# Attention ahead of two expert stages: full-row third score product, a shorter prologue, spread loads and splits

## The chip, the cores and the metric

The kernel runs on one core of a Trainium2 chip. The metric is the device time of one execution in microseconds (us), the median of several runs. Five engines work beside each other, each through its own list of instructions in order: TensorE (PE; weight loads are shown as PEld), VectorE (DVE), ScalarE (ACT), GpSimd (POOL) and SyncE (SP), which here issues the DMAs. Semaphores are the only order between engines.

## The reference

Three stages run in a row; only the first is touched by the change. It is attention with a position bias, over 2 batches, 8 heads, 576 positions and 64 columns per head:

```python
scores = scale * np.matmul(q, k.transpose(0, 1, 3, 2))
x = (psi_rel / psi_i)[..., None]            # from |i-j| and i
bias = np.maximum(x @ w1 + b1, 0.0) @ w2    # 32 hidden, one value per head
scores = scores + bias.transpose(2, 0, 1)[None]
attn = softmax(scores);  out = attn @ v
```

Then follow an MoE stage (1152 rows, 8 experts, 512 to 1024 to 512 columns) and an FFN (512 to 2048 to 512). Everything is float32.

## The kernel before, in words

A float32 product on TensorE is built from products of split operands: each operand is rounded to a short form ("h") and the rest is kept ("l"), and three of the products of parts are summed. For the scores the first two are one: a 128-row operand qs holds for each head h the rounded q in its 64 rows and q's rest in the other 64 rows, and meets kh, k's rounded copy in both halves. So one product over 128 rows yields two of the three. The third, q rounded with k's rest, is a product over 64 rows with kl.

Attention runs until about 214 us. A **block** is a pair of heads and a batch (8 blocks), a **step** is one block with one tile t of query rows (128 rows, or 64 for t = 4): 40 steps. The first four blocks go together, tile 4 first (steps 0 to 3), then tiles 0 to 3 of all four (steps 4 to 19); then come two groups of two blocks (steps 20 to 39).

Each step is written out by hand, one letter of an order string for each piece: R and S reduce the scores of the two heads with the bias (VectorE, L1213), E and F take the exponential (ScalarE, L1228), N norms (VectorE, and a spread of the reciprocals on POOL, L1239), T, U and V transpose the previous step's result, a is one of the five pieces of the value product (av, L1282, L1285, L1295), X writes the result back, Q is the next step's score product (sc, L1198 with kh, L1203 with kl). M, O and H are the bias: 36 **groups** of 16 rows, for each of which H computes four hidden rows ht (VectorE L1390 or ScalarE L1388), M multiplies them (TensorE, L1406), O scales them out and stores them to scr in HBM (L1441); L loads bias tiles bt of a step pair back from there (L1181). The string is ORD_A while bias groups are left, ORD_B after. A p takes one piece of a block's preparation (prep: two casts on VectorE, L1159, then subtractions on POOL, L1164 for qs and L1165 for kl) and two items of a background list.

The background list holds the splits of the first MoE weights (w_split, queued at steps 27 and 28; sums on POOL L302, copies on ScalarE L315, subtractions on VectorE L316) and of the first MoE operand (ops_first, queued at steps 35 and 37; POOL L332, ScalarE L352, VectorE L353).

Ahead of the steps stands a prologue of 12 groups, in which blocks 0, 1 and 2 are prepared (queued at groups 0, 2 and 6). The raw q and k of a block come by four DMAs into a ring of three places (load_qk). All DMAs are in SP's queue, in order. The MoE and FFN stages are ordered by a planner, from costs, after the attention; its inputs are the same before and after.

Of the kernel before, what the change touches and what calls it, by code (L numbers as in the profile page):

```python
# [7 lines left out]
F32 = mybir.dt.float32  # L8
# [14 lines left out]
HALF = S // 2  # L23
# [6 lines left out]
NB = 2  # L30
LAG = 1
TO = [4, 0, 1, 2, 3]
QB = 5
AB = 2
BD = 1
PRE = 12
PH = [0, 2, 6]
LQ = [4, 11, 105, 114, 116, 121]
LV = [1, 2, 3, 4, 20, 19, 32, 28]
ACC = [2.6, 3.1]  # L40
WARM = 8
PS = [[3, 0], [4, 12], [5, 16], [6, 19], [7, 25]]
ORD_A = "RXTSMOHUapaEaaNpFaLMOVQH"
ORD_B = "RTSNUXaafLEafappFVQa"
TOFF = [0, 128, 256, 384, 512]
TROW = [128, 128, 128, 128, 64]
NN = [256, 320]
# [172 lines left out]
def attention_moe_elu_ffn_kernel(  # L220
# [83 lines left out]
    def w_split():  # L304
        (kind, he, j), t = raw_q.pop(0)
        hi, lo = wt0[he, j] = w1_new()
        st = stp.tile([128, 4, 2, 128], F32, tag="st", name="st")

        def sums():
            for i in range(4):  # L310
                w1_sum(t, st, i, pool)

        def part(i):
            dst, src = w1_src(t, st)[i]
            act.activation(out=hi[:, dst], in_=src, func=ACTF.Copy)  # L315
            dve.tensor_tensor(out=lo[:, dst], in0=src, in1=hi.bitcast(F32)[:, dst], op=ALU.subtract)  # L316

        bg.extend([sums] + [lambda i=i: part(i) for i in range(4)] + [raw_load])

    def ops_new(n):  # L320
        p = xp if n == 0 else pools["ops1"]
# [19 lines left out]
    def ops_first(t):  # L341
        if not ops0:
            ops0.extend(ops_new(0))
        oh, ol = ops0
        i0, i1 = XPAIR[t]
        xa, xb = ops_view(0, t, xt[i0], xt[i1])
        c = slice(128 * t, 128 * t + 128)
        st = stp.tile([128, 4, 2, 128], F32, tag="st", name="st")

        def part(i):  # L350
            o, src = ops_src(xa, xb, st)[i]
            act.activation(out=oh[:, o, :, c], in_=src, func=ACTF.Copy)  # L352
            dve.tensor_tensor(out=ol[:, o, :, c], in0=src, in1=oh.bitcast(F32)[:, o, :, c], op=ALU.subtract)  # L353

        def sums(i):
            ops_sum(xa, xb, st, i, pool)
            ops_sum(xa, xb, st, i + 1, pool)

        bg.extend([lambda: sums(0), lambda: sums(2)] + [lambda i=i: part(i) for i in range(4)])

    plan = Plan(0.1)
    eng = {"A": act, "D": dve, "P": pool, "S": sp}
# [745 lines left out]
    left = ctx.enter_context(ExitStack())  # L1108

    def attention(fill):  # L1110
        qkp = sb("qk", QB, left)
        vpool = sb("v", 4, right, "right")
        ep = sb("e", LAG + 2, right, "right")
        atp = sb("attnT", AB, right, "right")
# [1 line left out]
        xfp = sb("xf", LAG + 1, right, "right")  # L1116
        bp = sb("bias", NB, left)
        up = sb("u", 1, left)
        op = sb("o", 4, left)
        ring = [xp.tile([128, 3, 2, S], F32, tag=t, name="ring") for t in ("oh0", "ol0")]  # L1120

        loaded = {}
# [10 lines left out]
        def load_qk(i):  # L1133
            hp, b = blocks[i]
            loaded[i] = []
            for src, rt in ((qt, ring[0]), (kt, ring[1])):
                r = rt[:, i % 3]
                for o in (0, 64):
                    sp.dma_start(out=r[o:o + 64], in_=src[b, hp])
                loaded[i].append(r)  # L1140

        def load_v(i):
            hp, b = blocks[i]
# [8 lines left out]
        def prep(i):  # L1152
            qs = qkp.tile([128, 2, S], F32R, tag="qs", name="qs")
            kh = qkp.tile([128, 2, S], F32R, tag="kh", name="kh")
            kl = qkp.tile([128, S], F32R, tag="kl", name="kl")
            prepped[blocks[i]] = qs, kh, kl
            qr, kr = loaded.pop(i)
            for dst, src in ((qs, qr), (kh, kr)):
                dve.tensor_copy(dst, src)  # L1159
                load["d"] += 0.73  # L1160
                yield
            for h in range(2):
                o, u = slice(64 - 64 * h, 128 - 64 * h), slice(64 * h, 64 * h + 64)
                pool.tensor_tensor(out=qs[o, h], in0=qr[o, h], in1=qs.bitcast(F32)[o, h], op=ALU.subtract)  # L1164
                pool.tensor_tensor(out=kl[u], in0=kr[u, h], in1=kh.bitcast(F32)[u, h], op=ALU.subtract)  # L1165
                yield

        def prep_next():
# [15 lines left out]
        def emit_qk(s):  # L1184
            hp, b, t = steps[s]
            qs, kh, kl = prepped[hp, b]
            r = TROW[t]
            etile[s] = (
                ep.tile([128, 2 * S], F32, tag="e", name="et"),
                tp.tile([128, 2], F32, tag="nmx", name="nmx"),  # L1190
                tp.tile([128, 2], F32, tag="sm", name="sm"),
            )
            sc = [psA("sc") for _ in range(2)]
            qc = slice(TOFF[t], TOFF[t] + r)
            for h in range(2):
                for x in range(2):
                    kc = slice(HALF * x, HALF * x + HALF)
                    pe.matmul(sc[h][0:r, x, 0:HALF], qs[:, h, qc], kh[:, h, kc], start=True, stop=False)  # L1198
            for x in range(2):
                for h in range(2):  # L1200
                    kc = slice(HALF * x, HALF * x + HALF)
                    hs = slice(64 * h, 64 * h + 64)
                    pe.matmul(sc[h][0:r, x, 0:HALF], qs[hs, h, qc], kl[hs, kc], start=False, stop=True)  # L1203
            for h in range(2):
                scs[s, h] = sc[h]

# [112 lines left out]
        def run_step(s):  # L1319
            d = s - LAG  # L1320
            cur, tr = s < NS, 0 <= d < NS
            for x in ORD_A if no[0] < GRP else ORD_B:
                if x == "T" and tr:
                    emit_tr(d, 0)
                elif x == "U" and tr:
                    emit_tr(d, 1)
                elif x == "V" and tr:
                    emit_trl(d)
                elif x == "Q" and s + 1 < NS:
                    emit_qk(s + 1)  # L1330
                elif x in "RS" and cur:
                    emit_ttr(s, "RS".index(x))
                elif x in "EF" and cur:
                    emit_exp(s, "EF".index(x))
                elif x == "N" and 1 <= s <= NS:
                    emit_norm(s - 1)
                elif x == "X":
                    x_evac()
                elif x == "a":
                    av(1)  # L1340
                elif x == "M":
                    bias_p()
                elif x == "O":
                    bias_o()
                elif x == "H":
                    bias_hh()
                elif x == "p":
                    prep_next()
                    do_bg(2)
                elif x == "L":  # L1350
                    bias_loads(s)
                elif x == "f":
                    fill_pe(s)
            if tr:
                av_q.extend(av_pieces(d))
# [6 lines left out]
            pe.matmul(wp[:, 0:128], ones, ones, start=True, stop=True)  # L1362
        sp.dma_start(out=csb, in_=cst)
        sp.dma_start(out=U, in_=lext)
        load_qk(0)
        load_qk(1)
        dve.tensor_scalar(bpsi, bpsi, csb[:, C_B1:C_B1 + 1], None, ALU.mult)
        dve.tensor_scalar(U, U, csb[:, C_W1:C_W1 + 1], None, ALU.mult)

# [46 lines left out]
        def bias_out():  # L1416
            g, ps = mq.pop(0)
            r0 = 16 * g
            mid = r0 + 15
            o = op.tile([128, S + 15], F32, tag="o", name="o")  # L1420
# [47 lines left out]
        for i in range(PRE):  # L1468
# [3 lines left out]
                bias_p(True)  # L1472
            bias_loads(0)
            if i in LQ:
                load_qk(2 + LQ.index(i))
# [5 lines left out]
        bias_o()  # L1481
        emit_qk(0)
        for s in range(NS + LAG):
            if 100 + s in LQ:
                load_qk(2 + LQ.index(100 + s))
            if s in LV:
                load_v(LV.index(s))
            for i, s0 in PS:
# [104 lines left out]
```

## Time and profile before

| what | us |
|---|---|
| median of 3 runs | 1208.25 (1206.49 to 1209.31) |
| the profiled execution | 1207.91 |
| its span | 1206.1 |
| PE busy | 1170.9 (97%) |
| DVE busy | 916.1 (76%) |
| ACT busy | 626.4 (52%) |
| POOL busy | 92.9 (8%) |

Rows of the trace carry the engine, the line of the kernel, the operation, out<-in and the shape, and a time in us unless a column says ns. In a timeline, the first column is the start and the second the stretch to the end of the last instruction of the row; rows of pipelined work overlap a little, so the distance from one start to the next is what a piece takes.

### The profile page before, as it was taken

What the parts mean: (1) busy time and instruction counts of PE and PEld (TensorE: products, weight loads), DVE (VectorE), ACT (ScalarE), POOL (GpSimd) and SP (SyncE); (2) the same over time, 40 slices, a digit from 0 to 9 for tenths busy, and PEclk for the clock granted to TensorE, in tenths of its full rate; (3) what the DMA queues carried; (4) which work ended last, traced back from release to release, by engine and by line L of the source; (5) the groups of instructions that cost most, each with busy time, mean ns of one, the idle gap of its engine ahead of it and who ended that gap; (6) DMA issues with size and microseconds to landing.
All of it is one profiled execution on the core that took longest, in us unless ns stands there. A gap on an engine that the chain in (4) does not pass through costs nothing.

```text
span 1206.1 us, 19661 instructions
## 1 busy us (share of the span) xinstructions
PE 1170.9 (97%) x7432; PEld 986.9 (82%) x7432; DVE 916.1 (76%) x1932; ACT 626.4 (52%) x1413; POOL 92.9 (8%) x107
## 2 busy tenths in 40 slices
PE   7899999999999999999999999999999988999998
PEld 3467777788888888888888888888888876788887
DVE  8987787664587778778788787787776468788875
ACT  6797667554333444443434444444434346777763
POOL 4402453000000000000000000000000001000000
PEclk9999999899999999999999999999999999999999
DMA  8767741111112233242232323232411101111102
GB/s 227 221 213 200 208 122 35 33 56 53 36 36 79 80 88 102 67 129 76 92 106 88 105 87 104 90 100 68 130 45 53 53 1 36 53 53 36 36 1 79
DMA packets 36285, 104.78 MB, mean 87 GB/s; under 512 B 4064, under 2 KB 4192, under 8 KB 36192
## 3 DMA queue, kind: packets, MB, share of 16 engines
q1 hardware_dynamic: 36192, 103.54, 28.5%
q8 instruction: 58, 0.95, 0.3%
q14 instruction: 35, 0.29, 0.1%
HBM read 81.88 MB, written 21.64 MB: 86 GB/s over the span
## 4 chain that ended last, share of the span: by engine, by line
PE 91%; DVE 3%; ACT 1%; POOL 1%; issue 0%; DMA 0%; ACTq 0%; DVEq 0%
PE y L717 41%; PE m L530 38%; PE av L1285 3%; PE tr L1254 2%; PE bps L1406 2%; PE sc L1198 1%; PE sc L1203 1%; PE av L1295 1%; PE trl L1266 1%; PE av L1282 1%; PE lg L873 0%; DVE ol L353 0%; DVE et L1213 0%; DVE w1l L316 0%; DVE ol L430 0%
## 5 line engine op out<-in xcount | busy, mean ns | idle before, releaser
L530 PE MATMUL m<-oh,w1h 128*128 128x256 f32 (+1 forms) x1120 | 335.8, 300 | 3.8 <-DVE c L562 1.4
L530 PE MATMUL m<-oh,w1l 128*128 128x256 f32 (+1 forms) x1120 | 330.6, 295 | 3.8 <-ACT u L543 1.6
L530 PE MATMUL m<-ol,w1h 128*128 128x256 f32 (+1 forms) x1120 | 330.3, 295 | 2.6 <-DVE c L562 1.3
L717 PE MATMUL y<-w2h,hh 128*128 128x512 f32 x720 | 284.6, 395 | 2.9 <-ACT hh L637 1.5
L717 PE MATMUL y<-w2h,hl 128*128 128x512 f32 x720 | 283.4, 394 | 0.0
L717 PE MATMUL y<-w2l,hh 128*128 128x512 f32 x720 | 282.5, 392 | 0.8 <-DVE w2l L430 0.8
L530 PEld LDWEIGHTS m<-oh,w1h 128*128 128x128 f32 x1120 | 211.0, 188 | 45.8 <-ACT u L543 13.3
L530 PEld LDWEIGHTS m<-ol,w1h 128*128 128x128 f32 x1120 | 211.4, 189 | 22.4 <-DVE c L562 1.9
L530 PEld LDWEIGHTS m<-oh,w1l 128*128 128x128 f32 x1120 | 211.3, 189 | 5.6 <-ACT u L543 2.3
L717 PEld LDWEIGHTS y<-w2h,hh 128*128 128x128 f32 x720 | 135.1, 188 | 18.8 <-ACT hh L637 2.3
L717 PEld LDWEIGHTS y<-w2h,hl 128*128 128x128 f32 x720 | 135.1, 188 | 17.8
L543 ACT ACTIVATE p<-m 128x256 f32<-128x256 f32 (+1 forms) x160 | 65.8, 411 | 161.3 <-PE m L530 157.3
L717 PEld LDWEIGHTS y<-w2l,hh 128*128 128x128 f32 x720 | 135.2, 188 | 16.2 <-DVE w2l L430 1.4
L543 ACT ACTIVATE u<-m 128x256 f32<-128x256 f32 (+1 forms) x160 | 65.9, 412 | 132.0 <-PE m L530 128.7
L593 ACT ACTIVATE hh<-c 128x512 fp32r<-128x512 f32 (+3 forms) x128 | 72.1, 563 | 109.7 <-DVE c L562 109.6
L748 DVE SCALAR_TENSOR_TENSOR acc<-y,P,acc 128x512 f32<-128x512 f32 x126 | 94.5, 750 | 37.3 <-PE y L717 35.4
L596 DVE SCALAR_TENSOR_TENSOR hl<-c,hh 128x512 fp32r<-128x512 f32 (+3 forms) x128 | 77.5, 605 | 20.4 <-ACT hh L593 18.6
L562 DVE TENSOR_TENSOR c<-m,u 128x256 f32<-128x256 f32 (+1 forms) x80 | 36.6, 458 | 73.7 <-PE m L530 72.0
L1213 DVE CUSTOM_DVE_ANT_0 et<-sc,bt 128x576 f32<-128x576 f32 (+1 forms) x80 | 57.9, 751 | 22.0 <-PE sc L1203 17.3
L332 POOL TENSOR_TENSOR st<-xt,st 128x256 f32<-128x256 f32 (+1 forms) x8 | 6.7, 835 | 755.2 <-DVE st L332 755.0
L1228 ACT ACTIVATE et<-et,nmx 128x576 f32<-128x576 f32 (+1 forms) x80 | 61.3, 771 | 3.2 <-DVE nmx L1213 3.1
L423 ACT ACTIVATE w2h<-raw 128x512 fp32r<-128x512 f32 x80 | 48.6, 625 | 21.7 <-PE y L717 12.4
(136 smaller groups left out, 1600.1 us busy)
## 6 DMA issues: line engine op xcount, KB each, us to landing
raw<-w1p SPq DMA_DIRECT2D x32, 512.0 KB, 3.6
raw<-w2p SPq DMA_DIRECT2D x32, 512.0 KB, 3.6
scr<-o SPq DMA_DIRECT2D x36, 295.5 KB, 3.5
bt<-scr SPq DMA_DIRECT2D x16, 576.0 KB, 4.9
cw<-w1d SPq DMA_DIRECT2D x16, 512.0 KB, 4.4
wsc<-ca SPq DMA_DIRECT2D x32, 256.0 KB, 4.4
cw<-w2d SPq DMA_DIRECT2D x16, 512.0 KB, 4.4
raw<-wsc SPq DMA_DIRECT2D x16, 512.0 KB, 3.6
```

The lines of the kernel that those rows point to most:

```text
L423: act.activation(out=dst(bh.get()), in_=src(), func=ACTF.Copy)
L530: lambda e, w=w, o=o, j=j, k=k: pe.matmul(x["ap"](bank), w.get()[:, ai, j, :], o.get()[:, bi, j, :], start=(k == 0 and i in (1, 2, 5)), st ...
L543: lambda e: act.activation(out=b.get()[:, 0:N], in_=x["ap"](bank), func=ACTF.Copy),
L562: lambda e: eng[e].tensor_tensor(out=blk(b.get()[:, half * N:half * N + N], rev), in0=ap(p), in1=ap(q), op=ALU.add),
L593: op([("A", cA(w))], lambda e: act.activation(out=hh(), in_=ap(), func=ACTF.Relu), r=sk, w=wh, after=gate_)
L596: lambda e: dve.scalar_tensor_tensor(out=bl.get()[:, d], in0=ap(), scalar=0.0, in1=hhf(), op0=ALU.max, op1=ALU.subtract),
L717: lambda e, a=a, w=w, f=f, i=i, y=y, c=c: pe.matmul(y.get(), a.get()[:, c], w.get(), start=(f == 0 and i == 0), stop=(f == 3 and i == 2)),
L748: lambda e: dve.scalar_tensor_tensor(out=a.get(), in0=y.get(), scalar=P[0][:, n, e_:e_ + 1], in1=a.get(), op0=ALU.mult, op1=ALU.add),
L1213: dve.tensor_tensor_reduce(out=e.rearrange("p (x j) -> p x j", x=2), in0=sc[0:r, :, 0:HALF], in1=biast[hp, t][0:r, h].rearrange("p (x j) - ...
L1228: act.activation(out=e, in_=e, func=ACTF.Exp, scale=-1.0, bias=nmx[0:r, h:h + 1], accum_out=sm[0:r, h:h + 1])
L1254: pe.transpose(p[:, 128 * j:128 * j + r], et[0:r, c0:c0 + 128], ident[0:r, 0:r])
L1285: pe.matmul(p[64 * h:64 * h + 64, 0:r], vt[:, j - 1, 64 * h:64 * h + 64], a[:, 4 * h + j - 1, 0:r], start=False, stop=(j == 4), skip_group ...
```

## The change

The third score product runs over all 128 rows: kl holds both heads' halves in the same layout as kh, its two POOL subtractions cover 128 partitions each, and the preparation has six pieces. The prologue has 8 groups and prepares blocks 0 and 1; steps 0 to 2 have an order of their own with three groups each, and blocks 2 and 3 are prepared wholly within steps 1 and 2, three pieces at each p. Blocks 4 to 7 are loaded by one DMA per step. In ORD_B the last value piece stands ahead of V and Q. A p takes one background item, and each item does the subtraction of the part before beside the copy of the next. The o tiles of the bias come from the pools of the weights.

```diff
-QB = 5
+QB = [5, 4]
-PRE = 12
-PH = [0, 2, 6]
-LQ = [4, 11, 105, 114, 116, 121]
-LV = [1, 2, 3, 4, 20, 19, 32, 28]
+PRE = 8
+PH = [0, 3]
+LQ = [4, 100]
+LS = [5, 9, 13, 21]
+LV = [0, 1, 2, 3, 19, 20, 28, 32]
-PS = [[3, 0], [4, 12], [5, 16], [6, 19], [7, 25]]
+PS = [[2, 1], [3, 2], [4, 13], [5, 16], [6, 20], [7, 26]]
+ORD_S = "RXTSMOHUapaMOHEaaNpFaLMOVQH"
 ORD_A = "RXTSMOHUapaEaaNpFaLMOVQH"
-ORD_B = "RTSNUXaafLEafappFVQa"
+ORD_B = "RTSNUXaafLEafaappFVQ"
...
         def part(i):
-            dst, src = w1_src(t, st)[i]
-            act.activation(out=hi[:, dst], in_=src, func=ACTF.Copy)
-            dve.tensor_tensor(out=lo[:, dst], in0=src, in1=hi.bitcast(F32)[:, dst], op=ALU.subtract)
-        bg.extend([sums] + [lambda i=i: part(i) for i in range(4)] + [raw_load])
+            if i:
+                dst, src = w1_src(t, st)[i - 1]
+                dve.tensor_tensor(out=lo[:, dst], in0=src, in1=hi.bitcast(F32)[:, dst], op=ALU.subtract)
+            if i < 4:
+                dst, src = w1_src(t, st)[i]
+                act.activation(out=hi[:, dst], in_=src, func=ACTF.Copy)
+        bg.extend([sums] + [lambda i=i: part(i) for i in range(5)] + [raw_load])
...
-            kl = qkp.tile([128, S], F32R, tag="kl", name="kl")
+            kl = klp.tile([128, 2, S], F32R, tag="kl", name="kl")
...
             for h in range(2):
-                o, u = slice(64 - 64 * h, 128 - 64 * h), slice(64 * h, 64 * h + 64)
+                o = slice(64 - 64 * h, 128 - 64 * h)
                 pool.tensor_tensor(out=qs[o, h], in0=qr[o, h], in1=qs.bitcast(F32)[o, h], op=ALU.subtract)
-                pool.tensor_tensor(out=kl[u], in0=kr[u, h], in1=kh.bitcast(F32)[u, h], op=ALU.subtract)
+                yield
+            for h in range(2):
+                pool.tensor_tensor(out=kl[:, h], in0=kr[:, h], in1=kh.bitcast(F32)[:, h], op=ALU.subtract)
                 yield
...
             for h in range(2):
-                for x in range(2):
-                    kc = slice(HALF * x, HALF * x + HALF)
-                    pe.matmul(sc[h][0:r, x, 0:HALF], qs[:, h, qc], kh[:, h, kc], start=True, stop=False)
-            for x in range(2):
-                for h in range(2):
-                    kc = slice(HALF * x, HALF * x + HALF)
-                    hs = slice(64 * h, 64 * h + 64)
-                    pe.matmul(sc[h][0:r, x, 0:HALF], qs[hs, h, qc], kl[hs, kc], start=False, stop=True)
+                for w, last in ((kh, False), (kl, True)):
+                    for x in range(2):
+                        kc = slice(HALF * x, HALF * x + HALF)
+                        pe.matmul(sc[h][0:r, x, 0:HALF], qs[:, h, qc], w[:, h, kc], start=not last, stop=last)
...
-            for x in ORD_A if no[0] < GRP else ORD_B:
+            for x in ORD_S if s < 3 else ORD_A if no[0] < GRP else ORD_B:
...
                 elif x == "p":
-                    prep_next()
-                    do_bg(2)
+                    for _ in range(3 if s < 4 else 1):
+                        prep_next()
+                    do_bg(1)
...
+            for i, s0 in enumerate(LS):
+                if s == s0:
+                    ld[0] = load_qk(4 + i)
+                if s0 <= s < s0 + 5:
+                    next(ld[0], None)
```

ops_first's parts are paired in the same way as those of w_split.

## Rows read from the trace of the kernel before

**Rows 1.** The page's chain that ended last: share of the span by engine.

```profile
PE 91%; DVE 3%; ACT 1%; POOL 1%; issue 0%; DMA 0%; ACTq 0%; DVEq 0%
```

**Rows 2.** Windows by stage: busy us (instructions) of each engine, clock, DMA share, GB/s.

```profile
31.60:54.10 22.50, 18.95 (x136) 8.93 (x135) 20.46 (x48) 15.89 (x40) 11.88 (x9) 0.92 0.75 229
...
105.00:161.30 56.30, 56.30 (x538) 44.56 (x536) 44.01 (x131) 36.25 (x105) 27.12 (x30) 1.00 0.72 193
161.30:178.30 17.00, 15.35 (x146) 11.09 (x146) 14.97 (x40) 13.28 (x39) 10.79 (x14) 1.00 0.44 135
```

**Rows 3.** Timeline of TensorE over one late step: start, length, line, operation, count.

```profile
111.96 0.33 PE L1266 MATMUL trl<-csb,et 128*128 128x128 f32 x1
112.05 0.78 PE L1198 MATMUL sc<-kh,qs 128*128 128x288 f32 x4
112.75 0.53 PE L1203 MATMUL sc<-kl,qs 64*128 64x288 f32 x4
113.22 0.44 PE L1285 MATMUL av<-aT,vt 128*64 128x128 f32 x4
113.59 0.33 PE L1295 MATMUL av<-csb,rcb 128*128 128x128 f32 x1
113.75 1.04 PE L1254 MATMUL tr<-csb,et 128*128 128x128 f32 x8
114.62 0.39 PE L1282 MATMUL av<-aT,vt 128*128 128x128 f32 x2
114.94 0.88 PE L1285 MATMUL av<-aT,vt 128*64 128x128 f32 x12
115.75 0.33 PE L1266 MATMUL trl<-csb,et 128*128 128x128 f32 x1
```

**Rows 4.** Timeline of TensorE in a step with bias groups.

```profile
86.11 1.10 PE L1285 MATMUL av<-aT,vt 128*64 128x128 f32 x16
87.14 0.33 PE L1295 MATMUL av<-csb,rcb 128*128 128x128 f32 x1
87.39 0.93 PE L1406 MATMUL bps<-ht,csb 128*32 128x432 f32 x8
```

**Rows 5.** Chain of waits, a piece of a late step: start, length, what.

```profile
178.52 0.54 PE sc L1198 x4
```

**Rows 6.** Timeline of VectorE in the first steps.

```profile
34.05 0.74 DVE L1213 CUSTOM_DVE_ANT_0 et<-sc,bt 64x576 f32<-64x576 f32 x1
...
40.42 0.75 DVE L1213 CUSTOM_DVE_ANT_0 et<-sc,bt 64x576 f32<-64x576 f32 x1 [1.97 <-PE sc L1203]
...
43.15 0.74 DVE L1159 CAST kh<-ring 128x1152 fp32r<-128x1152 f32 x1
...
52.52 0.74 DVE L1213 CUSTOM_DVE_ANT_0 et<-sc,bt 64x576 f32<-64x576 f32 x1
```

**Rows 7.** Timeline of SP's queue: the first bias loads.

```profile
24.08 1.29 SPq L1181 DMA_DIRECT2D bt<-scr  x2
```

**Rows 8.** All loads of bias tiles, in the tile's view: from issue to landing.

```profile
DMA to landing us min/median/max: 3.8/4.5/10.3
```

**Rows 9.** Two lines' views: duration in ns min/median/max over all their instructions.

```profile
L1164 POOL TENSOR_TENSOR qs<-ring,qs x16: 1410/1438/2377, 8.6 to 160.3; 64x576 fp32r<-64x576 f32 x16
...
L1390 DVE TENSOR_SCALAR ht<-U,csb x93: 366/448/1700, 4.7 to 100.5; 128x352 f32<-128x352 f32 x7, 128x496 f32<-128x496 f32 x6, 128x416 f32<-128x416 f32 x6, 128x400 f32<-128x400 f32 x6
```

**Rows 10.** The page's costliest groups: busy us, mean ns of one, idle before.

```profile
L332 POOL TENSOR_TENSOR st<-xt,st 128x256 f32<-128x256 f32 (+1 forms) x8 | 6.7, 835 | 755.2 <-DVE st L332 755.0
```

**Rows 11.** Windows of 2 us, columns as in rows 2.

```profile
36.00:38.00 2.00, 1.51 (x8) 0.53 (x8) 2.00 (x6) 0.46 (x2) 0.03 (x1) 0.63 0.99 312
...
214.00:216.00 2.00, 2.00 (x17) 1.73 (x14) 0.99 (x3) 0.42 (x2) 0.00 (x0) 0.50 0.00 0
```

**Rows 12.** Chain of waits, pieces of the weight split and of the tail.

```profile
165.68 3.19 DVE w1l L316 x3
...
205.96 1.89 DVE ol L353 x2
```

More of the change, by code (lines that the diff above doesn't have):

```diff
@@ L350, in part @@
         def part(i):
-            o, src = ops_src(xa, xb, st)[i]
-            act.activation(out=oh[:, o, :, c], in_=src, func=ACTF.Copy)
-            dve.tensor_tensor(out=ol[:, o, :, c], in0=src, in1=oh.bitcast(F32)[:, o, :, c], op=ALU.subtract)
+            if i:
+                o, src = ops_src(xa, xb, st)[i - 1]
+                dve.tensor_tensor(out=ol[:, o, :, c], in0=src, in1=oh.bitcast(F32)[:, o, :, c], op=ALU.subtract)
+            if i < 4:
+                o, src = ops_src(xa, xb, st)[i]
+                act.activation(out=oh[:, o, :, c], in_=src, func=ACTF.Copy)
         def sums(i):
@@ L357, in sums @@
             ops_sum(xa, xb, st, i + 1, pool)
-        bg.extend([lambda: sums(0), lambda: sums(2)] + [lambda i=i: part(i) for i in range(4)])
+        bg.extend([lambda: sums(0), lambda: sums(2)] + [lambda i=i: part(i) for i in range(5)])
     plan = Plan(0.1)
@@ L1110, in attention @@
     def attention(fill):
-        qkp = sb("qk", QB, left)
+        qkp, klp = sb("qk", QB[0], left), sb("kl", QB[1], left)
         vpool = sb("v", 4, right, "right")
@@ L1118, in attention @@
         up = sb("u", 1, left)
-        op = sb("o", 4, left)
         ring = [xp.tile([128, 3, 2, S], F32, tag=t, name="ring") for t in ("oh0", "ol0")]
@@ L1139, in load_qk, with load_now @@
                     sp.dma_start(out=r[o:o + 64], in_=src[b, hp])
+                    yield
                 loaded[i].append(r)
+        def load_now(i):
+            for _ in load_qk(i):
+                pass
         def load_v(i):
@@ L1162, in prep @@
             for h in range(2):
-                o, u = slice(64 - 64 * h, 128 - 64 * h), slice(64 * h, 64 * h + 64)
+                o = slice(64 - 64 * h, 128 - 64 * h)
                 pool.tensor_tensor(out=qs[o, h], in0=qr[o, h], in1=qs.bitcast(F32)[o, h], op=ALU.subtract)
-                pool.tensor_tensor(out=kl[u], in0=kr[u, h], in1=kh.bitcast(F32)[u, h], op=ALU.subtract)
+                yield
+            for h in range(2):
+                pool.tensor_tensor(out=kl[:, h], in0=kr[:, h], in1=kh.bitcast(F32)[:, h], op=ALU.subtract)
                 yield
@@ L1364, in attention @@
         sp.dma_start(out=U, in_=lext)
-        load_qk(0)
-        load_qk(1)
+        load_now(0)
+        load_now(1)
         dve.tensor_scalar(bpsi, bpsi, csb[:, C_B1:C_B1 + 1], None, ALU.mult)
@@ L1419, in bias_out @@
             mid = r0 + 15
-            o = op.tile([128, S + 15], F32, tag="o", name="o")
+            if g % 4 < 3:
+                o = rawp.tile([128, 1024], F32, tag="raw", name="o")[:, 0:S + 15]
+            else:
+                o = stp.tile([128, 4, 2, 128], F32, tag="st", name="o").rearrange("p i k f -> p (i k f)")[:, 0:S + 15]
             ip = csb[:, C_IPSI + g:C_IPSI + g + 1]
@@ L1474, in attention @@
             if i in LQ:
-                load_qk(2 + LQ.index(i))
+                load_now(2 + LQ.index(i))
             if i in PH:
@@ L1481, in attention @@
         bias_o()
+        bias_loads(0)
         emit_qk(0)
+        ld = [None]
         for s in range(NS + LAG):
             if 100 + s in LQ:
-                load_qk(2 + LQ.index(100 + s))
+                load_now(2 + LQ.index(100 + s))
+            for i, s0 in enumerate(LS):
[3 more added lines that the diff above has]
+                    next(ld[0], None)
             if s in LV:
```

## The prediction

> **What bounds the kernel now.** I read the page's chain of waits first: TensorE carries 91% of it [rows 1]. Its clock is full in the stages below but for two places, of which more in parts 2 and 4 [rows 11]. Everything from 221 us on is the MoE and FFN work; the planner and its order are not touched, so I carry it over unchanged. The reader should next see, in the windows by stage, that attention has three regimes [rows 2]. Up to 54 us VectorE is the bound (20.46 of 22.50 us busy, TensorE 18.95). From 105 to 161 us TensorE is busy for the whole stretch and VectorE is not. From 161 to 178 us TensorE has holes again. So a saving on TensorE is worth its full size only where the second regime holds, and work moved into the early steps is paid in VectorE time.
>
> **1. Third score product and the last output piece.** One late step runs from its trl transpose at 111.96 to the next at 115.75: 3.79 us, all TensorE [rows 3]. Taken by the starts of the groups: trl .09, four kh products .70, four kl products .47, four value products .37, the reciprocal's transpose .16, eight transposes .87, the two 128-row value products .32, twelve value products .81. After the change the kl products have the kh ones' shape, and the sixteen value products stand together, as they do in an earlier step already: 86.11 to 87.14, 1.03 us, then .25 for the reciprocal's transpose [rows 4]. The four kh products by themselves are .54 of chain time [rows 5], .135 each; the .16 that the row above has in excess stands before the next shape of tile. Eight at .135 are 1.08. The step after: trl .09, scores 1.08, transposes .87, .32, 1.03, and .16 to .25 for the reciprocal's transpose, 3.55 to 3.64; with .53 for four score products and the lower end, 3.53. So it saves .15 to .26; I take .22. Three of the five changes of tile shape go (at some .16 each), and the third product's .30 becomes .54. Steps that end on TensorE: 19 from 105 to 161 and 178 to 193 us and, with the stalls of part 4 mended, some 6 more: 25 × .22 = **−5.5**; bounds −3.8 and −6.5. In the steps with bias groups sc is eight products beside one shape change less: 1.16 becomes 1.14, nothing.
>
> The Trainium skill, TensorEngine Tiling (Array Packing), Key Properties, says that a change of tiling mode drains the array, which the .16 us at each change agrees with; the same page's Theoretical Speedup promises up to twice the rate where the contract dimension is 64 or less, and that is what this change gives up. By the second rule alone the step would grow by .24 us and part 1 would come to +6; that is rival D.
>
> **2. Bias groups, prologue and the first three steps.** Before, the first score reduction starts at 34.05, that of step 1 at 40.42, that of step 3 at 52.52 [rows 6]. With four groups fewer ahead of it, step 0 waits for the bias tile: its load is issued at 24.08 [rows 7] and lands some 4.5 us on, the median [rows 8]: 28.6, so −5.4. Step 0 then holds three groups rather than one and I reckon 8.1 us for it (before 6.4): reduction of step 1 at 36.7. Steps 1 and 2 each prepare a whole block. In the order of the instructions: two reductions 1.4; the first three hidden rows about 1.1; the copy of transposes .35; the casts .75 each [rows 6], of which only the first stands before a POOL operation; then on POOL one qs operation, the spread of the reciprocals (some .4, an estimate by its size), and three operations in a row, which the next score product waits for (behind it on TensorE stand only the third group's bias products, so all of TensorE waits); then the last two products and the reduction, .5. A POOL operation of this stage has a median of 1.44, I take 1.5; VectorE's hidden row goes from a median of 448 ns to 1700 beside one [rows 9]. The step is 1.4 + 1.1 + .35 + .7 + 1.5 + .4 + 4.5 + .5 = 10.5; with locked hidden rows among them up to 11.4. I take 11.0, twice: the reduction of step 3 at 58.7, **+6.1**. Before, steps 1 and 2 took (52.52 − 40.42)/2 = 6.05 each.
>
> The bounds. Low: POOL hides behind VectorE's own work of such a step: reductions 1.4, nine hidden rows at .45, casts 1.4, copy and norm .7, two outputs 1.0, some waits: 9.1 a step, so 36.7 + 18.2 = 54.9, **+2.4**. High: kl now spans 128 partitions, which no row shows for this type; the nearest is 128x256 at 835 ns [rows 10], which by columns (576 to 256) gives 1.88 us, and up to 2.6 where it shares with VectorE. Two of these a step add .8 to 2.2, twice: **+8 to +11**. The mean row of the 64-partition form is nearest in every other respect, so I keep the same 1.5.
>
> Also here: of the 36 groups 17 are done after step 2 before and 16 after; both kernels end them in step 12, so one more group falls into the stretch that TensorE bounds: eight products .93 [rows 4] plus shape changes, **+1.3** (bounds 0 and 1.5). Idle TensorE in steps 1 and 2 also brings the lower clock: 36 to 38 us shows .63 now [rows 11], behind a wait of TensorE for the reduction of step 0. Two longer pauses, each with some 3 us of work at the 1.2 GHz level behind it, of which half is on the path: **+1.4**, bounds 0 and +3.
>
> The Trainium skill, SBUF — State Buffer, SBUF: two separate sides, has it that VectorE and GpSimd share one pair of ports, as a lock that is held for a whole instruction. The 448 against 1700 ns of the hidden row agree. By it, POOL operations that VectorE has no work beside cost VectorE nothing, which would put part 2 nearer to its low bound.
>
> **3. Loads one per step.** Blocks 4 to 7 are loaded by four single DMAs in steps 5 to 8, 9 to 12, 13 to 16, 21 to 24, and prepared from 13, 16, 20 and 26. On SP each stands behind the bias stores and one bias load of its step, where before four stood in a row; every block's load ends about as its preparation begins or before, and the product that needs it is two steps on: 0. If one were late, its casts would hold VectorE's queue, the reductions behind them, for some 4 us, a landing time; the bounds are 0 and +4. Block 3's load is issued at step 0 and read in step 2, 16 us later: 0.
>
> **4. Splits spread.** From step 28 on ScalarE's copy and VectorE's subtraction of the same quarter stand behind each other, two quarters at each p, and the chain shows it: 3.19 us of w1l subtractions, three of 1.06 [rows 12], with TensorE behind. The four steps at 161 to 178 us take 17.0 us, 15.35 of them busy on TensorE [rows 2]; two of them have 64-row tiles, and at an estimated 3.5 us a step (3.79 for a full one) they would be 14, 3.0 us less. With one item at each p a subtraction stands behind a copy made half a step before; I leave .7 of the 3.0: **−2.3** (bounds 0 and −3). Two more places: steps 36 to 38 lose a like stall, **−.5**, and at the tail the two ol subtractions, 1.89 us, stand before the last reduction [rows 12], and ScalarE's copies of the same parts behind it; with some .6 for these, **−2.5** (bounds 0 and −4). What is late next there is the remaining items, which the filler now does at the end: four of one copy and one subtraction, beside the last value products. The clock at the start of MoE is at half, .50 from 214 us on [rows 11], the 1.2 GHz level, behind TensorE's waits in the tail. With shorter gaps a part of this goes: **−1.0**, bounds 0 and −3.
>
> **5. o tiles from other pools.** Still four in rotation, and these pools are free until step 20: 0.
>
> **The sum**, on the profiled execution's own 1207.91 us (span 1206.1): −5.5 + 6.1 + 1.3 + 1.4 − 2.3 − .5 − 2.5 − 1.0 = −3.0, thus 1204.9. The median of the runs shown, 1208.25, is .34 above that execution: **1205.2 us**. A change is told from none here at about 0.2%, 2.4 us.
>
> **Rivals.**
> B, the early chain is hidden: part 2's low bound and no half clock there. For: VectorE's own work is nearly as long as POOL's chain. Against: the three POOL operations in a row have only one group's rows to stand behind. −5.5 + 2.4 + 1.3 − 6.3 = −8.1: 1200.2 us.
> C, slower: kl over 128 partitions in steps 1 and 2 is the price. Decides if one kl operation is above about 2.3 us: +11 in place of +6.1, with the rest as forecast, +1.9, and the clock's upper bound +1.6: 1211.7 us. For: the 835 ns of a 128-partition operation of under half the columns. Against: in the stage's own form 576 elements cost 1.44.
> D, slower or none: the late step isn't shorter, as the drains come back elsewhere (the last value piece stands before trl, not away from it), or the eight products at full width cost .24 more with no drain saved. −5.5 becomes 0 to +6: 1210.7 us at 0. For: half the array did two products at once. Against: the sixteen value products together, in [rows 4].
> E, the split's items land where the tail can't hide them: four items on ScalarE and VectorE after the last step, −2.5 becomes +1: 1208.7.
>
> **How the numbers follow.** Forecast .42, its own range 1202.5 to 1208; B .25; C .13; D .10; E .10. Faster by more than 2.4 us (below 1205.8): .24 of the forecast's .42, and nearly all of B: .49. Slower: C and D, .23, and a little of E: .25. Within: the rest, .26. The range for 8 in 10 runs from a little below B to C, 1198.5 to 1211.5.
>
> **What would show it.** The late step: 3.55 to 3.6 us from trl to trl, with the sc products in one row of eight. The early steps: reductions at 28.6, 36.7, 47.7, 58.7, and POOL as the releaser of sc; a step under 9 us is B, a kl operation above 2.3 us is C. The last bias product near 105 us plus 7.4. The stretch behind it with holes of under .7 us. The first MoE product 2.0 us earlier than now, and its clock at full level for part of the 6 us behind it. Wrong altogether if the stretch from 221 us on changes by more than 1 us, as nothing here counts on it.

## The result, and the profile after

The changed kernel takes 1215.8 us (median of 5 runs, 1212.4 to 1216.5 but for one), against 1208.45 us before: a ratio of 1.0056, 95% interval [1.0038, 1.0075]. It is slower by some 7 us where 3 us less were forecast, and outside the forecast range. One execution of it, the first that was profiled, took 1927 us, with a granted clock of .56 from 241 us on, and one of the kernel before took 1880 us later; neither is used below. The rows of after are from a further run of the changed kernel (span 1212.6 us, in that run 1.0065 [1.0042, 1.0089] of before).

The windows by stage of the changed kernel, columns as in [rows 2]:

```profile
31.60:66.00 34.40, 27.13 (x137) 10.58 (x137) 30.94 (x51) 19.22 (x45) 16.94 (x12) 0.65 0.55 168
...
112.00:168.30 56.30, 56.23 (x561) 48.30 (x555) 48.43 (x137) 40.94 (x113) 23.55 (x27) 1.00 0.65 192
168.30:186.00 17.70, 17.44 (x181) 15.30 (x179) 15.54 (x45) 13.02 (x40) 11.05 (x13) 1.00 0.42 116
```

The late stages hold: TensorE has 561 products in 56.3 us where it had 538, and the weight split no longer leaves holes (17.44 of 17.70 busy). The loss is early, and its sign is the clock column: .65 from 31.6 to 66 us, where the answering window of [rows 2] had .92. VectorE's timeline of the first steps, answering [rows 6] (the first reduction of steps 0 to 4, and the longest row between):

```profile
29.83 0.75 DVE L1223 CUSTOM_DVE_ANT_0 et<-sc,bt 64x576 f32<-64x576 f32 x1 [4.02 <-DMA bt<-scr]
...
39.87 0.75 DVE L1223 CUSTOM_DVE_ANT_0 et<-sc,bt 64x576 f32<-64x576 f32 x1 [2.36 <-PE sc L1213]
...
46.21 5.18 DVE L1401 TENSOR_SCALAR ht<-U,csb 128x432 f32<-128x432 f32 x3
51.31 0.74 DVE L1223 CUSTOM_DVE_ANT_0 et<-sc,bt 64x576 f32<-64x576 f32 x1
...
63.63 0.74 DVE L1223 CUSTOM_DVE_ANT_0 et<-sc,bt 64x576 f32<-64x576 f32 x1
...
71.95 0.75 DVE L1223 CUSTOM_DVE_ANT_0 et<-sc,bt 128x576 f32<-128x576 f32 x1
```

POOL's timeline in step 1:

```profile
46.36 0.52 POOL L1249 TENSOR_TENSOR rcb<-ones,rc 64x128 f32<-64x128 f32 x1 [0.29 <-DVE rc L1247]
46.85 1.42 POOL L1176 TENSOR_TENSOR qs<-ring,qs 64x576 fp32r<-64x576 f32 x1
48.24 2.90 POOL L1179 TENSOR_TENSOR kl<-ring,kh 128x576 fp32r<-128x576 f32 x2
```

And TensorE's, with windows of 2 us (the granted clock is the third number from the end):

```profile
47.59 0.48 PE L1213 MATMUL sc<-kh,qs 128*64 128x288 f32 x2
49.68 0.48 PE L1213 MATMUL sc<-kl,qs 128*64 128x288 f32 x2 [1.61 <-POOL kl L1179]
49.99 0.58 PE L1213 MATMUL sc<-kh,qs 128*64 128x288 f32 x2
51.20 0.74 PE L1213 MATMUL sc<-kl,qs 128*64 128x288 f32 x2 [0.62 <-POOL kl L1179]
```

```profile
48.00:50.00 2.00, 0.39 (x4) 0.32 (x4) 2.00 (x2) 1.41 (x4) 2.00 (x3) 1.00 0.19 74
50.00:52.00 2.00, 1.38 (x7) 0.56 (x6) 2.00 (x4) 0.00 (x0) 1.14 (x1) 0.53 0.84 241
52.00:54.00 2.00, 2.00 (x12) 0.57 (x12) 1.78 (x7) 0.39 (x1) 0.00 (x0) 0.50 0.00 0
...
72.00:74.00 2.00, 2.00 (x16) 1.17 (x14) 1.99 (x8) 0.38 (x1) 0.00 (x0) 0.50 0.42 160
74.00:76.00 2.00, 2.00 (x32) 1.35 (x25) 1.62 (x7) 1.39 (x4) 0.26 (x1) 1.00 0.00 0
...
222.00:224.00 2.00, 1.96 (x19) 1.70 (x20) 1.95 (x4) 1.31 (x4) 0.00 (x0) 1.00 0.00 0
```

So POOL's qs, kl, kl in a row hold two things: TensorE, which has .39 us of work in 2 us, and VectorE, whose three hidden rows take 5.18 us (the longest 3.32 us). Behind that wait TensorE runs at .50, its 1.2 GHz level, for 24 us (50 to 74), though it is busy for nearly all of them; step 3, with no preparation in it, takes 8.3 us. The start of the MoE stage, at .50 before [rows 11], now has the full clock (the last row above).

The first reduction of step 13, the first step behind the last bias group, starts at 122.4 us (before 106.2: +16.2):

```profile
122.37 0.76 DVE L1223 CUSTOM_DVE_ANT_0 et<-sc,bt 128x576 f32<-128x576 f32 x1 [1.70 <-PE sc L1213]
```

The first MoE product starts at 221.5 (214.05: +7.5), and the end of the span comes 6.5 us later.

### The profile page after: what moved, and what is told of

Same layout as the page of the kernel before. It is cut to its first block, busy times and chain, and to the rows that moved or that the text cites. A ratio compares the mean times of both kernels' runs of the same rounds, so it can differ in the third digit from the quotient of the medians.

```text
span 1925.5 us, 19673 instructions
## 1 busy us (share of the span) xinstructions
PE 1896.8 (99%) x7432; PEld 1370.5 (71%) x7432; DVE 927.9 (48%) x1932; ACT 630.0 (33%) x1414; POOL 87.2 (5%) x107
## 4 chain that ended last, share of the span: by engine, by line
PE 96%; POOL 0%; issue 0%; ACT 0%; DVE 0%; DVEq 0%; ACTq 0%; POOLq 0%
PE y L725 43%; PE m L538 38%; PE sc L1213 4%; PE av L1295 3%; PE tr L1264 3%; PE bps L1417 2%; PE av L1292 1%; PE av L1305 1%; PE lg L881 0%; PE trl L1276 0%; PE x2t L975 0%; POOL kl L1179 0%; POOL qs L1176 0%; DVE c L570 0%; ACT u L551 0%
## 5 line engine op out<-in xcount | busy, mean ns | idle before, releaser
L538 PE MATMUL m<-ol,w1h 128*128 128x256 f32 (+1 forms) x1120 | 459.5, 410 | 1.8 <-DVE c L570 1.3
L538 PE MATMUL m<-oh,w1h 128*128 128x256 f32 (+1 forms) x1120 | 457.1, 408 | 3.4 <-ACT p L551 1.4
L538 PE MATMUL m<-oh,w1l 128*128 128x256 f32 (+1 forms) x1120 | 455.5, 407 | 3.8 <-ACT u L551 1.6
L725 PE MATMUL y<-w2h,hh 128*128 128x512 f32 x720 | 414.4, 576 | 1.7 <-ACT hh L645 1.0
L725 PE MATMUL y<-w2l,hh 128*128 128x512 f32 x720 | 415.9, 578 | 0.0
L725 PE MATMUL y<-w2h,hl 128*128 128x512 f32 x720 | 413.9, 575 | 0.0
L538 PEld LDWEIGHTS m<-ol,w1h 128*128 128x128 f32 x1120 | 254.3, 227 | 98.8 <-issue 49.7
L538 PEld LDWEIGHTS m<-oh,w1l 128*128 128x128 f32 x1120 | 258.4, 231 | 25.6 <-ACT u L551 2.7
L1223 DVE CUSTOM_DVE_ANT_0 et<-sc,bt 128x576 f32<-128x576 f32 (+1 forms) x80 | 60.2, 755 | 85.4 <-PE sc L1213 80.0
L1417 PE MATMUL bps<-ht,csb 128*32 128x512 f32 (+17 forms) x352 | 65.9, 814 | 9.8 <-ACT ht L1399 4.4
L1264 PE MATMUL tr<-csb,et 128*128 128x128 f32 (+1 forms) x320 | 72.2, 397 | 0.0
```

The costliest lines, as they stand in the source:

```text
L538: lambda e, w=w, o=o, j=j, k=k: pe.matmul(x["ap"](bank), w.get()[:, ai, j, :], o.get()[:, bi, j, :], start=(k == 0 and i in (1, 2, 5)), st ...
L725: lambda e, a=a, w=w, f=f, i=i, y=y, c=c: pe.matmul(y.get(), a.get()[:, c], w.get(), start=(f == 0 and i == 0), stop=(f == 3 and i == 2)),
L1223: dve.tensor_tensor_reduce(out=e.rearrange("p (x j) -> p x j", x=2), in0=sc[0:r, :, 0:HALF], in1=biast[hp, t][0:r, h].rearrange("p (x j) - ...
L1264: pe.transpose(p[:, 128 * j:128 * j + r], et[0:r, c0:c0 + 128], ident[0:r, 0:r])
L1417: pe.matmul(p[32 * c:32 * c + 32, d0 - lo:d1 - lo], csb[:, C_W2:C_W2 + 32], ht[c][:, d0:d1], start=True, stop=True, tile_position=(0, 32 * c),
```

## The experiments

Each ratio is to the kernel before, with its 95% interval. "Step 13" is the start of its first reduction in the trace, 106.2 before and 122.4 in the changed kernel. The first run is the one shown above.

> The changed kernel once more, for a trace: the first one stood at about half the clock for its whole length and tells little of single terms. Theory 1 (the start): the mean granted clock is near .98, as in the timed runs, and the stretches at half clock stand in the first 70 us, behind TensorE's idle time in steps 0 to 2; the step from 105 us on is shorter by .2 us, the reduction of step 3 is at 64 us or later. Theory 2 (the full-row product, or the denser late steps, bring the clock down): the half-clock stretches stand behind 105 us, in the late steps or in the MoE stage, and the late step is no shorter there. Either way about 1212 to 1217 us.

1217.2 us in two runs. The half-clock stretches were at 26 to 40 and 50 to 74 us (and for 3 us in the prologue), and none between there and 1029 us: theory 1.

**The start undone.**

```diff
-PRE = 8; PH = [0, 3]; LQ = [4, 100]; PS = [[2, 1], [3, 2], ...
+PRE = 12; PH = [0, 2, 6]; LQ = [4, 11]; PS = [[3, 0], ...
-ORD_S if s < 3 else ORD_A if ...      # three prep_next at a p
+ORD_A if ...                          # one; two prep_next a group
-bias_loads(0)                         # the load just ahead of step 0
```

> The changed kernel with the start of before: 12 groups in the prologue with blocks 0 to 2, block 3 in steps 0 to 2, ORD_A from step 0. Full-row product, last value piece, one background item at a time and single loads stay. Theory 1 (the start is what costs): the clock comes back to .99 or more and the time falls to 1196 to 1203 us, below before. Theory 2 (product or late steps bring the clock down): it stays at 1211 to 1217 us with a mean clock of .98.

1204.9 us, 0.996 [0.9945, 0.9974], mean clock .995, step 13 at 109.6. Theory 1: the rest of the change is a gain, the start alone turns it. It came out 2 us above the expectation, as the first reduction was late (37.4); more on that below.

**The start alone**, in the kernel before (those lines the other way round).

> The kernel before with the new start alone: 8 groups in the prologue, three groups a step in steps 0 to 2, blocks 2 and 3 wholly in steps 1 and 2, with the old half-row product and its 64-partition kl. Theory 1: slower than before by 8 to 20 us (the early chain, one more group in step 12, and half clock), 1216 to 1228 us, mean clock .985 or less. Theory 2: within 6 us of before, up to 1214 us, mean clock .99 or more.

1232.3 us, 1.0186 [1.017, 1.0201], above even theory 1's range; half clock at 31 to 37 and 61 to 82 us, step 13 at 123.3. What goes beyond the range came later: with the old background the clock fell again at 187 to 201 us, and the stretch between the reductions of steps 28 and 32 took 21.2 us against 17.1 before.

**The product undone**: kl on 64 rows, four preparation pieces.

> The changed kernel with the third product back on 64 rows (kl on 64 partitions, preparation of four pieces). Theory 1: slower than the changed kernel by about 4 us less what the smaller kl saves in steps 1 and 2, so 1213 to 1221 us, with the mean clock still near .98. Theory 2: the clock comes back to .99 or more and the time falls to 1203 to 1209 us.

1222.4 us, 1.0106 [1.0089, 1.0123]: theory 2 falls. It is 1.4 us above theory 1's range because of something that was not foreseen. With four pieces, one block's qs, kl, qs, kl stand in POOL's queue ahead of the next step's spread of the reciprocals, and in step 16 TensorE waits for that:

```profile
140.05 0.47 PE L1307 MATMUL av<-csb,rcb 128*128 128x128 f32 x1 [3.46 <-POOL rcb L1251]
```

The last value piece reads the reciprocals, and the change has moved it ahead; with six pieces for these blocks, in all other runs with it, that wait is absent or at most .9 us.

**TensorE kept at work, too much of it.**

```diff
+# ahead of each bias product of steps 0 to 2 and of the score products of steps 1 to 3
+for _ in range(12):                    # 28 for the first, 14 for scores
+    pe.matmul(<the tile that is written next>, ones, ones, start=True, stop=True)
```

> The changed kernel with products of ones added on TensorE where it waited in steps 0 to 2: 28 ahead of the first bias product of step 0, 12 ahead of each of the eight others, 14 ahead of the score products of steps 1 to 3 (each 128x128, about .11 us at full clock); their results are overwritten. Theory 1a (of the start's price, the larger part is the clock that falls while TensorE waits): the half-clock stretches of 26 to 40 and 52 to 74 us go or shrink to a few us, step 3 falls from 8.3 to about 5 us, and the time falls by 5 to 9 us, to 1207 to 1212 us, though work was added. Theory 1b (the chain through POOL and VectorE is nearly all of it): the time stays within 2 us of the changed kernel's 1216 or rises by the added work, up to 1222.

1235.4 us, 1.0212 [1.0183, 1.0241]: neither expectation holds. The clock came back (mean .992, full from 34 to 242 us), but each float32 product is two instructions, so the added work was twice what I had reckoned and became the path itself. It was made smaller, below.

**Blocks 0 to 2 in the short prologue**, block 3 piece by piece over steps 0 to 2.

```diff
-PH = [0, 3]; LQ = [4, 100]; PS = [[2, 1], [3, 2], ...   # one prep_next a group, three at a p
+PH = [0, 2, 5]; LQ = [3, 6]; PS = [[3, 0], ...          # three a group, one at a p
```

> The changed kernel with blocks 0 to 2 prepared in its prologue of 8 groups, three pieces a group, and block 3 piece by piece over steps 0 to 2, two a step; three groups a step in steps 0 to 2 stay. Theory 1b (the POOL run inside steps 1 and 2 is the price, wherever the clock stands): the reduction of step 3 comes at 55 to 58 us instead of 63.6, and the time is 1200 to 1208 us. Theory 1c (three groups in a step, or eight in the prologue, are the price, wherever the blocks are prepared): the reduction of step 3 stays at 61 us or later, the time at 1212 us or more.

1205.5 us, 0.9966 [0.9949, 0.9984]; the reduction of step 3 at 57.6, no half clock from 25 us on but in the last 3 us, step 13 at 112.0. Moving the blocks out of steps 1 and 2 is worth 10.3 us at step 13, which refutes theory 1c and is in theory 1b's range. But the low clock went with the blocks, so this run can't tell the POOL run from the clock behind it; the runs with fewer added products do, below.

**The old start with the old pieces**: one cast, or one qs and kl pair, at a time for blocks 0 to 3.

```diff
                 pool.tensor_tensor(out=qs[o, h], ...)
+                if i < 4:
+                    pool.tensor_tensor(out=kl[:, h], ...)
                 yield
-            for h in range(2):
+            for h in range(2 if i >= 4 else 0):
```

> The kernel with the old start once more, but with blocks 0 to 3 prepared as before, one cast or one pair of POOL operations a piece and one piece a group, instead of two pieces a group. If the 3.4 us by which the old start's first reduction came late (37.4 against 34.05) are VectorE held behind longer POOL runs, it comes at 34 to 35 us here and the time is 1199 to 1203 us; if they are the wider kl, it stays at 37 us and 1203 to 1206 us.

1200.2 us, 0.992 [0.9894, 0.9945], the best of all: first reduction at 33.9, step 13 at 104.9. The wider kl costs nothing. But the 3.5 us between the two traces (37.45 and 33.89) are only in part VectorE behind longer POOL runs: its 28 hidden rows of the prologue take 22.0 us in the one and 21.3 in the other. VectorE's timeline in the old start with two pieces a group, and in this one, shows where the larger part lies:

```profile
9.99 1.81 DVE L1171 CAST kh<-ring 128x1152 fp32r<-128x1152 f32 x1 [1.78 <-DMA ring<-kt]
```

```profile
10.09 0.75 DVE L1171 CAST kh<-ring 128x1152 fp32r<-128x1152 f32 x1
```

With two pieces a group the first block's cast is asked for before its raw k has landed, and VectorE idles 1.7 us more in all; the cast itself then stands beside a POOL operation and takes 1.1 us more.

**kl of blocks 2 and 3 on VectorE** (`dve` for `pool` in their two subtractions).

> The changed kernel with the kl subtractions of blocks 2 and 3 on VectorE instead of POOL, in the same places. Theory 1b (the POOL run in steps 1 and 2): it is shorter by two operations a step, VectorE's hidden row of 4.3 us behind it goes, steps 1 and 2 fall from 11.4 and 12.3 to 9 to 10 us, TensorE waits less, and the time falls to 1203 to 1211 us. Theory 1c (three groups a step are the price): steps 1 and 2 stay above 11 us, as VectorE has 1.3 us more to do in each, and the time stays within 2 us of 1216.

1210.5 us, 0.9998 [0.9976, 1.002]; steps 1 and 2 at 10.3 and 9.8 us. Theory 1b for the two steps: the reduction of step 3 comes 3.5 us sooner (60.2). But at step 13 only 1.1 us of it is left in the trace (121.3): the clock still fell, later (62 to 79 us), and steps 3 and 4 took 7.0 and 8.3 us. The ten runs go with their mean clock: three at .992 or .993 took 1204 to 1206 us, six at .984 to .987 took 1210 to 1212.

**Fewer added products, sized to the holes**: 6, 3, 1 and 4 ahead of four bias products of steps 0 and 1, 6 ahead of the score product of step 2.

> The changed kernel with far fewer products of ones than in the run before, sized to the holes that TensorE has in steps 0 and 1: 6 and 3 ahead of the first two bias products of step 0, 1 and 4 ahead of two in step 1, 6 ahead of the score product of step 2 (two instructions of .12 us each, 4.8 us in all). Theory 1a (the lost clock is a large part): the half-clock stretch from 52 to 74 us goes or is cut to under 8 us, step 3 falls from 8.3 to 5 to 6 us, step 4 from 5.8 to 5.3, and the time falls by 4 to 8 us, to 1208 to 1212 us. Theory 1b (the chains of steps 0 to 2 are nearly all of it): it stays at 1214 us or more even if that stretch goes.

1213.6 us, 1.0029 [1.0006, 1.0052], step 13 at 119.7: between the two expectations. The clock now held until 62 us, but TensorE then waited for POOL in step 2, with none added there, and the clock fell behind that wait:

```profile
58.00:60.00 2.00, 0.41 (x3) 0.42 (x4) 2.00 (x2) 1.11 (x5) 2.00 (x3) 1.00 0.85 316
60.00:62.00 2.00, 1.23 (x13) 0.66 (x15) 2.00 (x5) 0.00 (x0) 1.03 (x1) 0.95 0.54 172
62.00:64.00 2.00, 2.00 (x13) 0.65 (x13) 1.69 (x6) 0.83 (x2) 0.00 (x0) 0.50 0.04 8
...
72.00:74.00 2.00, 2.00 (x31) 1.32 (x30) 1.60 (x6) 2.00 (x6) 0.40 (x1) 0.99 0.13 50
```

**That hole filled too**: 2 more ahead of the last bias product of step 2, 9 ahead of the score product of step 3.

> The changed kernel with the small products of ones, and more of them in step 2: 2 ahead of its last bias product and 9 ahead of the score product of step 3, where TensorE waits for POOL's kl. The run before it with none there kept a half-clock stretch from 61 to 73 us. If that stretch is the cause of the slow steps 3 and 4 (7.85 and 6.2 us), it goes, they take 4.8 to 5.4 us, the last bias step ends some 3 us earlier and the time falls to 1208 to 1211 us. If steps 3 and 4 are slow for another reason, they stay above 7 and 6 us, and the time at 1213 us or more.

1207.5 us, 0.9988 [0.9978, 0.9998], step 13 at 114.8; step 3 takes 5.5 us, step 4 4.3. This is the first expectation, or a little better. In the same windows, with the same POOL run still there:

```profile
60.00:62.00 2.00, 1.73 (x16) 0.83 (x17) 2.00 (x7) 0.38 (x1) 0.22 (x1) 1.00 0.23 89
62.00:64.00 2.00, 2.00 (x31) 1.37 (x30) 1.45 (x6) 1.94 (x4) 0.38 (x1) 1.00 0.08 32
...
72.00:74.00 2.00, 2.00 (x32) 1.51 (x31) 1.97 (x8) 1.90 (x5) 0.00 (x0) 1.00 0.82 252
```

```profile
114.80 0.76 DVE L1225 CUSTOM_DVE_ANT_0 et<-sc,bt 128x576 f32<-128x576 f32 x1 [1.69 <-PE sc L1215]
```

From 62 to 64 us TensorE has 31 products against 13, none of them an added one. Work whose result is thrown away brought back 7.6 us at step 13, and with it what the whole change had lost. In the span it is 6.5 us, as the start of the MoE stage fell back to half clock (214 to 221 us).

**The last value piece back**, in the best kernel.

```diff
-ORD_B = "RTSNUXaafLEafaappFVQ"
+ORD_B = "RTSNUXaafLEafappFVQa"
```

> The kernel with the old start and four preparation pieces (1200.2 us), with the last value piece back behind the score product in ORD_B. If moving the piece is .15 us of each late step, as the trace of the changed kernel with the 64-row product suggests (3.64 against 3.79 us), the late step is 3.70 us and the time 1203 to 1205 us. If the full-row product is what shortens the step, it stays at 3.57 us and the time at 1200 to 1201 us.

1204.1 us, 0.9944 [0.9924, 0.9963]: slower than the best by 4 us, the time of the first expectation, but the step is 3.85 us and not 3.70, longer than before the change. Its timeline:

```profile
146.26 0.33 PE L1278 MATMUL trl<-csb,et 128*128 128x128 f32 x1
146.35 0.51 PE L1215 MATMUL sc<-kh,qs 128*128 128x288 f32 x2
146.70 0.43 PE L1215 MATMUL sc<-kl,qs 128*128 128x288 f32 x2
146.96 0.42 PE L1215 MATMUL sc<-kh,qs 128*128 128x288 f32 x2
147.22 0.42 PE L1215 MATMUL sc<-kl,qs 128*128 128x288 f32 x2
147.58 0.44 PE L1297 MATMUL av<-aT,vt 128*64 128x128 f32 x4
147.95 0.33 PE L1307 MATMUL av<-csb,rcb 128*128 128x128 f32 x1
...
150.11 0.33 PE L1278 MATMUL trl<-csb,et 128*128 128x128 f32 x1
```

**The old background**: two items at each p, each a copy and a subtraction of the same part, in the best kernel.

> The kernel with the old start and four preparation pieces, with two background items at each p again, each with the copy and the subtraction of the same part. If the split's spreading is worth what was forecast for it (2.3 + .5 + 2.5 us and a part of the clock at the start of the MoE stage), the time is 1204 to 1207 us, with TensorE idle for about 3 us between the score products of steps 28 and 32. If the shorter late step hides the splits anyway, 1200 to 1202 us.

1211.3 us, 1.0008 [0.9992, 1.0024]: 11 us above the best, beyond both expectations. TensorE's hole in step 28 brought the lower clock with it:

```profile
162.00:164.00 2.00, 1.32 (x12) 0.97 (x9) 2.00 (x3) 0.26 (x1) 2.00 (x2) 1.00 0.01 4
164.00:166.00 2.00, 0.00 (x0) 0.00 (x0) 0.72 (x2) 0.75 (x2) 1.92 (x4) 1.00 0.00 0
166.00:168.00 2.00, 1.15 (x6) 0.87 (x6) 2.00 (x4) 1.39 (x6) 2.00 (x2) 0.77 0.23 35
168.00:170.00 2.00, 2.00 (x18) 1.61 (x17) 1.97 (x8) 2.00 (x5) 0.81 (x2) 0.50 0.77 252
...
178.00:180.00 2.00, 2.00 (x12) 1.98 (x10) 1.15 (x6) 0.75 (x3) 0.40 (x1) 0.50 0.79 311
```

**The product on 64 rows**, in the best kernel.

> The kernel with the old start and four preparation pieces, with the third product on 64 rows again (kl on 64 partitions, all else as it is). If the full-row product is .07 us a step, the late step is 3.63 us and the time 1201 to 1203 us; if it is the .2 us of the forecast by itself, 3.75 us and 1204 to 1206 us; if the two 64-row products at once were worth more than the two shape changes, the time falls below 1200 us.

1202.2 us, 0.9931 [0.9908, 0.9955]; the late step is 3.625 us (14.5 us from the reduction of step 22 to that of step 26). This is the first expectation, .07 us a step.

**Two groups a step** from step 0 on (ORD_A in place of ORD_S), in the kernel with blocks 0 to 2 in the short prologue.

> The kernel with blocks 0 to 2 prepared in a prologue of 8 groups (1205.5 us), with ORD_A, two groups a step, from step 0 on; the groups then end some two steps later. If three groups in a step are the price of the shorter prologue, the reduction of step 3 comes at 48 to 52 us and the time is 1199 to 1202 us. If a group costs the same wherever it stands, or more beside the steps than in the prologue, the time stays at 1204 to 1208 us.

1211.2 us, 1.0023 [1.0002, 1.0043], single runs from 1206 to 1217, of which the profiled one, at 1206.2, is the shortest. This is neither expectation: the reduction of step 3 came at 51.3, as in the first, but that of step 18, where both have all groups behind them, at 132.6 against 130.0 (with 12 groups in the prologue 127.6 at two pieces a group, 122.9 at one). This order brings a price of its own. The groups end two steps later, and behind step 3 three reductions waited for their bias tiles, 6.1 us in all, where the run with three groups a step has no such wait. The first and the last of them:

```profile
58.73 0.76 DVE L1223 CUSTOM_DVE_ANT_0 et<-sc,bt 128x576 f32<-128x576 f32 x1 [1.93 <-DMA bt<-scr]
...
126.16 0.76 DVE L1223 CUSTOM_DVE_ANT_0 et<-sc,bt 128x576 f32<-128x576 f32 x1 [2.43 <-DMA bt<-scr]
```

So in either order the four groups cost more beside the steps than in the prologue, even against 127.6, but whether three in a step are a price by themselves is not shown. Why the runs spread so is open.

## Why the prediction was wrong

**The step that failed** is the clock term of part 2: "Two longer pauses, each with some 3 us of work at the 1.2 GHz level behind it, of which half is on the path: +1.4, bounds 0 and +3." The mechanism was there; the size was not. The half-clock stretches were 14 and 24 us long, and filling TensorE's holes gave back 7.6 us at step 13 (122.4 to 114.8), net of the added products. Little of it came in the two steps where POOL's run sets the pace: .7 ahead of step 0, 1.7 in step 0, .9 in steps 1 and 2 together, 2.8 in step 3 and 1.5 in step 4. I had taken the length of a stretch from the one early row of before [rows 11], which ended some 3 us after it began. In the changed kernel TensorE stays at half clock for 24 us although it is busy in nearly all of them, and step 3 takes 8.3 us with no preparation in it.

With that term at 7.6 the forecast's 1205.2 becomes 1211.4; the start without the clock (1.2 more than forecast) and the late stages (2.1 less gain), both below, make it 1214.7, near the measured 1215.8. Point by point:

- Step 0: the first reduction at 29.8 (forecast 28.6), the next at 39.9 (36.7). That ORD_S has three groups "rather than one" was wrong, as ORD_A has two; the step was 10.0 us, not 8.1, all of it at half clock; with the added products, where the clock is full again from 33 us on, it took 8.3.
- Steps 1 and 2: 11.4 and 12.3 us (forecast 11.0), and 11.6 and 11.3 with the added products. The kl operation of 128 partitions took 1.45 us in the median, as the 64-partition one: rival C's condition is refuted, and so is B's, with steps above 9 us. The Trainium skill, SBUF — State Buffer, SBUF: two separate sides, has VectorE and GpSimd lock their shared ports for a whole instruction; the trace agrees: a hidden row of .45 us takes 1.6 beside a POOL operation. In step 1 and in step 2 one row took 3.3 us, across a qs operation and the kl behind it.
- What the start costs, by step 13: the runs, with one trace each, split the +16.2 us into −1.3 (the rest of the change, in the best kernel, 104.9), +7.1 for the shorter prologue with blocks 0 to 2 in it (112.0), +2.8 for blocks 2 and 3 inside the steps with most of the clock kept (114.8; some 10 us of half clock are left ahead of 47 us), and +7.6 for the clock (122.4). The +7.1 is not the four groups alone, as the preparation is packed too, three pieces a group in place of one: the first reduction comes only 1.2 us sooner than in the best kernel (32.7 against 33.9), and with 12 groups two pieces a group cost 4.7 us at step 13 (109.6 against 104.9). Without the clock that is +8.6, against +6.1 + 1.3 forecast.
- Part 1, .22 us a step: right. Late steps take 3.55 us, 143.11 to 146.66 in the changed kernel's timeline:

```profile
143.11 0.27 PE L1276 MATMUL trl<-csb,et 128*128 128x128 f32 x1
143.14 0.51 PE L1213 MATMUL sc<-kh,qs 128*128 128x288 f32 x2
143.49 0.42 PE L1213 MATMUL sc<-kl,qs 128*128 128x288 f32 x2
143.75 0.43 PE L1213 MATMUL sc<-kh,qs 128*128 128x288 f32 x2
144.02 0.43 PE L1213 MATMUL sc<-kl,qs 128*128 128x288 f32 x2
144.28 1.04 PE L1264 MATMUL tr<-csb,et 128*128 128x128 f32 x8
145.16 0.39 PE L1292 MATMUL av<-aT,vt 128*128 128x128 f32 x2
145.47 1.09 PE L1295 MATMUL av<-aT,vt 128*64 128x128 f32 x16
146.50 0.33 PE L1305 MATMUL av<-csb,rcb 128*128 128x128 f32 x1
146.66 0.27 PE L1276 MATMUL trl<-csb,et 128*128 128x128 f32 x1
```

  But it is the two edits together. The four cases stand at 3.79 (neither), 3.63 (the piece moved), 3.85 (the full rows alone) and 3.55 us (both): that is 5, 4, 4 and 2 changes of tile shape at .16 us, and .24 more for four full-row products. Rival D was right of the full rows alone. The Trainium skill, TensorEngine Tiling (Array Packing), has a drain at a change of tiling mode in Key Properties and up to twice the rate for 64 rows in Theoretical Speedup; the trace agrees with both, with .16 us a change and .30 against .54 us for four products. Which one wins here is a count of changes.
- From step 13 to the first MoE product: −8.7 us, and −1.0 behind it, together −9.7 against −11.8. The tail behind the last score product gave 1.6 and not 2.5. The MoE stage's first 6 us came to the full clock, as forecast.
- Part 4 was sized right for the changed kernel (the steps from 28 to 32 are 3.1 us shorter), but the spread is worth more than forecast in the shorter steps: 11 us by the medians in the best kernel. In the traces 9.3 us of it lie between the reductions of steps 28 and 32, where the clock fell.
- Loads of blocks 3 to 7: no wait showed. o tiles: one did, VectorE's 2.0 us at 24.9 us for a store; the first reduction waits for its bias tile until 29.8 behind it.

What stays open: how the 7.1 us divide between the packed preparation, the place of the four groups and their number in a step.

## What to carry to other kernels

Price a wait of TensorE by what runs behind it as well as by its own length: the lower clock can stay for many times the wait, and work that is thrown away, put into the hole, can be the cheaper choice (it cost 6.5 us less here in the span). Keep runs of small POOL operations off a chain of VectorE rows: beside them a row of .45 us took 1.6 us, and at two places 3.3. And count changes of tile shape over the whole loop before widening a product: the wider product alone lost .06 us a step, both edits together gained .24.

## What was not expected of the hardware

A POOL subtraction of 128x576 took as long as one of 64x576 (medians 1.446 and 1.438 us). The lower clock came behind a hole of 1.6 us and held for 24 us of nearly unbroken TensorE work; before, it had risen some 3 us on. A float32 product of 128 columns was two instructions of .11 us at full clock.
